# Reordering a turn of chunked linear attention: scores first, one row half for state and early value products

## The chip, the cores and the metric

The kernel runs on one core of a Trainium2 chip. The core has TensorE (PE, matmuls into PSUM), VectorE (DVE), ScalarE (ACT), GpSimdE (POOL), and SyncE (SP), which issues the transfers here. Each engine works through its own list in order; semaphores tie the lists together. The metric is the time of one execution on the device in microseconds (us).

## The reference, cut to what matters

A linear attention with a decaying state, then a dense MLP, then a mixture of experts. The change touches the attention alone:

```python
for t in range(S):
    kt, vt, rt = (k[:, :, t], v[:, :, t], r[:, :, t])
    cur = np.einsum('bhd,bhe->bhde', u[None] * kt, vt)
    y[:, :, t] = np.einsum('bhd,bhde->bhe', rt, state + cur)
    state = w[None, :, :, None] * state + np.einsum('bhd,bhe->bhde', kt, vt)
...
x = np.ascontiguousarray(attn_out.transpose(0, 2, 1, 3)).reshape(B * S, H * D)
x = _moe_ref(x=x, **moe_kwargs)
return _moe2_ref(x=x, **moe2_kwargs)
```

There are 4 batches, 8 heads, 768 tokens and a head dimension of 48; all matrices of the attention are fp32.

## The kernel before, in words

The tokens of a batch are cut into 6 chunks of 128, so there are 24 chunks, taken chunk by chunk over the 4 batches. r is scaled by falling powers of w (RT), k by rising ones (raw_p, KP in the code), so that inside a chunk the decay falls away: y of a chunk is scores times values, below the diagonal, plus a diagonal with u, plus RT times the state that came in. Heads are handled in four pairs j; s is the head in the pair. The first head of a pair has its 48 dimensions in partitions 0 to 47, the second in 64 to 111. Tokens come in two halves of 64 as well, so that most matmuls use one half of PE's rows and one half of its columns.

`turn(i)` issues the work of one step of the pipeline, and 25 turns run one after another, `merge`d with steps of the splitting of the MLP's weights (`load_weights`: mk and wah on ACT, four ti/tf steps on DVE, wal on POOL). PACE says how many steps each turn takes; a piece needs five, and a turn takes mostly four. On PE a turn consists of these blocks, named as the rest of this document names them:

- **state** (L436): RT of chunk i-1 times SW, the decayed state, into y
- **pk** (L402): transposes of the scaled k of chunk i+2; ACT copies the result to KT (`keep_k`)
- **kv** (L451): k times v of chunk i, which DVE adds to the state (Sn)
- **early products** (L464): those value products of chunk i-1 whose weights read the token half that lies in the first row half
- **sums** (L351): two columns per pair of u-weighted products of chunk i+1; ACT copies half of them to cs, then writes four diagonal blocks of AT (L368), and DVE the other four (`diagonal`)
- **late products** (L474): the value products with the other token half
- **scores** (L509): RT times KT of chunk i into pA

`masked` copies what is above the diagonal of pA over AT (a predicated copy on DVE) and the blocks between the token halves (on ACT). After the late products ACT copies y to ysb (L486), and SP writes that to DRAM (xd). y, pA, pk and kvc (kv and the sums) have one PSUM buffer each. Where two blocks write one bank of y from different row halves, `after` puts a drain on PE and waits for it:

```python
self.nc.tensor.drain().then_inc(self.tiles, 1)
self.nc.tensor.wait_ge(self.tiles, self.count)
```

State is left out in the first five turns (i up to 4), as the first chunk of each batch has none. `warm` issues matmuls of the identity whose result nobody reads. Ahead of turn 0 `att_setup` builds the powers TK and TR by doubling, and calls `warm` by the four numbers of WARM. Loads are issued by `load_chunk(i + 5)` after turn i.

Of the kernel before, what the change touches and what calls it, by code (L numbers as in the profile page):

```python
# [18 lines left out]
P = 128  # L19
# [4 lines left out]
NCB = S // P  # L24
# [20 lines left out]
EARLY = "k0 r0 k1 r1 w k2 r2 w k3 r3 w"  # L45
SLOTS = (0, 1, 2, 3, 5, 4, 7, 6)
WARM = (8, 10, 3, 2)
# [40 lines left out]
class Kernel:  # L88
# [20 lines left out]
    def consts(self):  # L109
# [6 lines left out]
        twice = cp.tile([P, P + 64], F32, name="ident")  # L116
        self.ident, self.swap = twice[:, :P], twice[:, 64:]
        v.tensor_scalar(self.ident, jp, 0.0, None, op0=ALU.is_equal)
        v.tensor_copy(twice[:, P:], twice[:, :64])
# [47 lines left out]
    def att_setup(self, ctx):  # L167
# [33 lines left out]
        for i in range(8):  # L201
            if i < 7:
                v.reciprocal(IW[:, i, :], PW[:, i, :])
                v.tensor_mul(PW[:, i + 1, :], PW[:, i, :], PW[:, i, :])
            if i == 0:
                g.tensor_copy(TR[:, :, 127], IW[:, 0, :])
            else:
                i -= 1
                n = 1 << i
                pb = PW[:, i, :].unsqueeze(2).to_broadcast([112, 4, n])  # L210
                ib = IW[:, i, :].unsqueeze(2).to_broadcast([112, 4, n])
                v.tensor_mul(TK[:, :, P - 2 * n:P - n], TK[:, :, P - n:], pb)
                g.tensor_mul(TR[:, :, P - 2 * n:P - n], TR[:, :, P - n:], ib)
# [5 lines left out]
        for j in range(4):  # L219
            if j < 2:  # L220
                nc.tensor.transpose(pt[:, j, :112], TK[:, j, :], self.ident[:112, :112])
            else:
                for c in range(2):
                    nc.tensor.matmul(pt[64 - 64 * c:P - 64 * c, j, :112], TK[:, j, 64 * c:64 * c + 64],
                                     self.ident[:112, :112], start=True, stop=True)
# [8 lines left out]
        self.kvc = self.pa.tile([P, 4 * D + H + 1], F32, tag="kv", name="kvc")  # L234
        self.pA = self.pa.tile([P, 2, 512], F32, tag="pA", name="pA")
        self.tiles, self.count = self.tc.alloc_semaphore("tiles"), 0
        self.scale_r(0)
        self.warm(WARM[2])
# [5 lines left out]
        self.warm(WARM[3])  # L244
# [36 lines left out]
    def warm(self, n, t=None):  # L281

        if n and t is None:
            t = self.pa.tile([P, P], F32, tag="kv", name="warm")
# [59 lines left out]
    def sums(self, prod, mark=False):  # L344
# [3 lines left out]
        for j in range(4):  # L348
            for c in range(2):
                d = 64 * (c if j < 2 else 1 - c)  # L350
                mm = self.nc.tensor.matmul(cc[d:d + 64, 2 * j:2 * j + 2], prod[:, j, 64 * c:64 * c + 64], self.uw[:, j, :],  # L351
                                           start=True, stop=True, skip_group_check=True)
                if mark and j == 0 and c:
                    self.ordered(mm)

    def diagonal(self, i):
# [6 lines left out]
        AT = self.AT[i] = self.wk.tile([P, 2, 384], F32, name="AT", bufs=3)  # L363
        sh = [P, 4, 64]
        nc.vector.tensor_tensor(AT[:, 1, :256].rearrange("p (j t) -> p j t", j=4), self.i64.unsqueeze(1).to_broadcast(sh),
                                cc[:, 1::2].unsqueeze(2).to_broadcast(sh), op=ALU.mult)
        for j in range(4):
            nc.scalar.mul(AT[:, 0, 64 * j:64 * j + 64], self.i64, cs[:, j:j + 1])  # L368
# [27 lines left out]
    def turn_k(self, i, **kw):  # L396
# [4 lines left out]
        for j in range(4):  # L401
            self.nc.tensor.transpose(pk[:, j, :], KP[:, j, :112], self.ident if j < 2 else self.swap)  # L402

    def keep_k(self, i):
# [3 lines left out]
        self.nc.scalar.copy(KT, self.pk)  # L408
# [7 lines left out]
    def turn(self, i):  # L416
# [6 lines left out]
        if cur:  # L423
            KV, KP = self.raw["k", i % NRAW["k"]], self.raw["p", i % NRAW["p"]]
        if prev:
            self.masked(i - 1)
            y = self.pa.tile([112, 2, 512], F32, tag="y", name="y")
            side = lambda j, s: 64 * (s if j < 2 else 1 - s)
            place = lambda j, s, o: y[side(j, s):64 if side(j, s) == 0 else 112, j // 2, P * (j % 2) + o:P * (j % 2) + P]
            width = lambda j, s: D if side(j, s) else 64  # L430
            RTp = self.RT.pop(i - 1)
            if pc:
                for j in (0, 2, 1, 3):
                    for s in range(2):
                        o = slice(64 * s, 64 * s + D)
                        nc.tensor.matmul(place(j, s, 0), self.SW[o, pb, j * D:j * D + width(j, s)], RTp[o, j, :],  # L436
                                         start=(j % 2 == 0), stop=False, skip_group_check=True)
# [4 lines left out]
        if prev and pc < NCB - 1:  # L442
            g.tensor_mul(self.SW[:, pb, :4 * D].rearrange("p (j d) -> p j d", j=4),
                         self.Sn[(i - 1) % 2].rearrange("p (j d) -> p j d", j=4), self.WC)
        kv = None
        if cur and c < NCB - 1:
            kv = self.kvc[:112, :4 * D]
            for j in range(4):
                for q, m in enumerate((64, D)):
                    h = 2 * j + q  # L450
                    mm = nc.tensor.matmul(kv[64 * q:64 * q + m, j * D:j * D + D], KP[:, h, :m], KV[:, h * D:h * D + D],  # L451
                                          start=True, stop=True, skip_group_check=True)
        yield
        prod = self.prod.pop(i + 1, None)
        if prev:
            Vp, ATp = self.raw["k", (i - 1) % NRAW["k"]], self.AT.pop(i - 1)
            if pc:
# [1028 lines left out]
```

## Time and profile before

| | |
|---|---|
| median of 3 runs | 855.35 us (854.48 to 858.29) |
| the profiled execution | 857.5 us |
| its span on the core | 855.7 us |
| mean granted clock of TensorE over the span | 0.898 |
| attention stage | to about 187 us of the span |

The span runs from the first to the last instruction that the profiler saw. The granted clock is a share of 2.4 GHz; its lower level, 1.2 GHz, reads 0.50. Matmul rows of one block overlap, so the length of a block is best read as the distance from its start to the start of the next. A product or transpose of fp32 may stand as more records than instructions.

### The profile page before, as it was taken

The numbers are of one execution on the slowest core, as the hardware profiler recorded it, in microseconds if no ns is written. First come the engines' busy times: TensorE is split into PE (matmuls) and PEld (weight loads), VectorE is DVE, ScalarE is ACT, GpSimd is POOL, SyncE is SP. The second block draws the span as 40 slices with busy tenths as digits, with TensorE's granted clock in tenths as the row PEclk, the third lists the DMA queues.
The fourth block names the chain that finished last, engine by engine and source line by source line (L and its number), as shares of the span: only waits on it lengthen the run. The fifth ranks groups of instructions, "written<-read, shape, count | busy, mean of one in ns | idle before, by whom it ended". The sixth has DMA issues, their size and how long they took to land.

```text
span 855.7 us, 17300 instructions
## 1 busy us (share of the span) xinstructions
PE 819.8 (96%) x6539; PEld 738.2 (86%) x6539; DVE 571.9 (67%) x1583; ACT 393.4 (46%) x861; POOL 269.3 (31%) x269
## 2 busy tenths in 40 slices
PE   8889899989999999999999999999899999999996
PEld 7777777768999999889999999998889999999996
DVE  5644544539879899998898843466868777875221
ACT  4543443446664444444444444563254544444441
POOL 6535335313230000000000000000295867777771
PEclk8655555559999999999999999999999999999998
DMA  8645346324502002002002001000553355327400
GB/s 250 160 149 172 110 142 184 120 59 148 171 15 74 1 1 75 0 10 93 28 20 83 11 1 56 1 21 10 170 191 115 97 196 205 129 91 233 159 29 29
DMA packets 56362, 81.42 MB, mean 95 GB/s; under 512 B 6990, under 2 KB 42064, under 8 KB 56144
## 3 DMA queue, kind: packets, MB, share of 16 engines
q1 hardware_dynamic: 53168, 70.81, 26.4%
q0 software_dynamic: 3104, 9.44, 3.3%
q8 instruction: 53, 0.87, 0.4%
q14 instruction: 37, 0.30, 0.1%
HBM read 66.08 MB, written 14.16 MB: 94 GB/s over the span
## 4 chain that ended last, share of the span: by engine, by line
PE 64%; DVE 5%; issue 3%; POOL 2%; ACT 2%; DMA 1%; POOLq 0%; ACTq 0%; DVEq 0%; SPq 0%
PE m L691 23%; PE ph L750 21%; PE eph L1238 8%; PE o L1255 8%; PE cnt L903 1%; DVE G L898 1%; POOL wal L1198 1%; PE ept L1222 1%; PE eph L286 1%; POOL wbl L1198 1%; DVE gh L765 1%; POOL out_dram L1268 1%; DMA xg<-md,idx 1%; ACT nt L754 0%; PE ip L1008 0%
## 5 line engine op out<-in xcount | busy, mean ns | idle before, releaser
L750 PE MATMUL ph<-xh,wah 128*128 128x512 f32 (+1 forms) x336 | 123.1, 366 | 1.0 <-ACTq L259 0.8
L750 PE MATMUL ph<-xh,wal 128*128 128x512 f32 (+1 forms) x336 | 122.7, 365 | 0.0
L750 PE MATMUL ph<-xl,wah 128*128 128x512 f32 (+1 forms) x336 | 122.7, 365 | 0.0
L691 PE MATMUL m<-wbh,gl 128*128 128x384 f32 (+1 forms) x352 | 119.3, 339 | 0.1
L691 PE MATMUL m<-wbl,gh 128*128 128x384 f32 (+1 forms) x352 | 119.2, 339 | 0.0
L691 PE MATMUL m<-wbh,gh 128*128 128x384 f32 (+1 forms) x352 | 119.1, 338 | 0.0
L754 ACT ACTIVATE nt<-ph 128x512 f32<-128x512 f32 (+1 forms) x112 | 60.1, 537 | 121.5 <-PE ph L750 115.5
L765 DVE SCALAR_TENSOR_TENSOR gt<-nt,al,gt 128x512 f32<-128x512 f32 (+1 forms) x96 | 67.7, 705 | 53.0 <-ACT gt L755 53.0
L773 ACT CAST gh<-gt 128x512 fp32r<-128x512 f32 (+1 forms) x96 | 56.4, 587 | 72.1 <-DVE gt L765 72.1
L147 POOL MEMSET io<- 128x1 f32 x1 | 0.1, 98 | 253.1 <-DVE io L146 253.1
L1241 ACT ACTIVATE hh<-eph 128x384 fp32r<-128x384 f32 x64 | 31.5, 492 | 103.8 <-PE eph L1238 99.8
L1246 DVE SCALAR_TENSOR_TENSOR hl<-eph,hh 128x384 fp32r<-128x384 f32 x64 | 35.4, 554 | 59.7 <-ACT hh L1241 59.4
L615 DVE SCALAR_TENSOR_TENSOR junk<-wt,wgb 128x384 f32<-128x384 f32 x128 | 71.3, 557 | 3.9
L750 PEld LDWEIGHTS ph<-xh,wal 128*128 128x128 f32 x336 | 63.8, 190 | 11.0
L750 PEld LDWEIGHTS ph<-xh,wah 128*128 128x128 f32 x336 | 63.7, 189 | 9.4 <-ACTq L259 0.9
L750 PEld LDWEIGHTS ph<-xl,wah 128*128 128x128 f32 x336 | 63.7, 190 | 7.7
L776 DVE TENSOR_TENSOR gl<-gt,gh 128x512 fp32r<-128x512 f32 (+1 forms) x96 | 61.7, 643 | 12.7 <-ACT gh L773 12.6
L691 PEld LDWEIGHTS m<-wbl,gh 128*128 128x128 f32 x352 | 66.1, 188 | 3.6
L691 PEld LDWEIGHTS m<-wbh,gh 128*128 128x128 f32 x352 | 66.1, 188 | 3.5
L691 PEld LDWEIGHTS m<-wbh,gl 128*128 128x128 f32 x352 | 66.1, 188 | 0.4 <-DVE gl L776 0.4
L1198 POOL TENSOR_TENSOR wbl<-raw,wbh 128x768 fp32r<-128x768 f32 x32 | 58.4, 1848 | 20.3 <-ACT wbh L1194 20.2
L1198 POOL TENSOR_TENSOR wal<-raw,wah 128x768 fp32r<-128x768 f32 x32 | 58.3, 1845 | 18.2 <-ACT wah L1194 17.0
(274 smaller groups left out, 1821.8 us busy)
## 6 DMA issues: line engine op xcount, KB each, us to landing
raw<-in_moe_w_dram SPq DMA_DIRECT2D x64, 384.0 KB, 5.8
raw_k<-in_kv_dram SPq DMA_DIRECT2D x24, 384.0 KB, 4.3
raw<-in_moe_w_in_dram SPq DMA_DIRECT2D x16, 384.0 KB, 4.3
raw<-in_moe_w_out_dram SPq DMA_DIRECT2D x16, 384.0 KB, 3.1
raw_r<-in_rt_dram SPq DMA_DIRECT2D x24, 224.0 KB, 4.5
xd<-ysb SPq DMA_DIRECT2D x48, 96.0 KB, 2.1
md<-raw SPq DMA_DIRECT2D x22, 192.0 KB, 2.0
xr<-xd SPq DMA_DIRECT2D x15, 256.0 KB, 4.0
```

Of the source, the lines that this page charges most:

```text
L615: v.scalar_tensor_tensor(junk, t, 1.0, self.wgb[:, e], op0=ALU.mult, op1=ALU.mult, accum_out=wc[:, f, e:e + 1])
L691: nc.tensor.matmul(acc[t][:, :N], a[:, o], self.wb[b][:, f, :N], start=(f == 0 and n == 0), stop=(f == NF - 1 and n == 2))
L750: nc.tensor.matmul(ph[:, :T], self.wa[a][:, k, fs], b[:, k, :T], start=(n == 0), stop=(n == 8))
L754: nc.scalar.activation(nt[:, :T], ph[:, :T], AF.Relu, scale=-1.0)
L765: v.scalar_tensor_tensor(gt[:, :T], nt[:, :T], self.al[:, f:f + 1], gt[:, :T], op0=ALU.mult, op1=ALU.add)
L773: nc.scalar.copy(h, g)
L776: v.tensor_sub(l, g, h.bitcast(F32))
L1198: self.nc.gpsimd.tensor_sub(to[1], d, to[0].bitcast(F32))
L1238: self.nc.tensor.matmul(ph, w1[a][:, k, f * P:(f + 1) * P], x[b][:, k], start=(n == 0), stop=(n == 8))
L1241: self.nc.scalar.activation(hh, ph, AF.Relu)
L1246: self.nc.vector.scalar_tensor_tensor(hl, ph, 0.0, hh.bitcast(F32), op0=ALU.max, op1=ALU.subtract)
L1255: self.nc.tensor.matmul(self.acc[q], h[a][:, o], w2[b][:, f], start=(f == 0 and n == 0), stop=(f == NS - 1 and n == 2))
```

## The change

Within a turn, scores(i) go from the end to the head, masked(i) follows in the same turn (before: masked(i-1) at the head of turn i), early products move up behind state, and sums stand ahead of kv. For the second head of each pair the two token halves of r, k and v are exchanged when the arrays are laid out, so that state and early products of one head use the same row half and the same bank of y; state of that head is issued in two pieces of 64 columns. The drains go, except in the last three turns. The late products, which come from the other row half, wait for the KT copy (`keep_k`) of the turn instead. AT and pA are laid out flat, so that one predicated copy of 512 elements does the work of two of 256. FILL adds 16 unread matmuls in turns 0 to 2. EARLY loads k and r of chunk 2 ahead of the first weight piece. The last doubling of TK and TR is split into a copy on ACT and two products each; `ident` replaces a second, shifted identity. In `scores` and `sums` only the places of the results differ.

```diff
-EARLY = "k0 r0 k1 r1 w k2 r2 w k3 r3 w"
-SLOTS = (0, 1, 2, 3, 5, 4, 7, 6)
-WARM = (8, 10, 3, 2)
+EARLY = "k0 r0 k1 r1 k2 r2 w k3 r3 w w"
+SLOTS = (0, 5, 2, 7, 1, 4, 3, 6)
+WARM = (8, 10, 4, 3)
+FILL = {(0, 0): 5, (0, 1): 3, (1, 0): 5, (2, 0): 3}
...
@@ -209,20 +208,20 @@
-                v.tensor_mul(TK[:, :, P - 2 * n:P - n], TK[:, :, P - n:], pb)
-                g.tensor_mul(TR[:, :, P - 2 * n:P - n], TR[:, :, P - n:], ib)
+                for e, t, b in ((v, TK, pb), (g, TR, ib)):
+                    if i < 6:
+                        e.tensor_mul(t[:, :, P - 2 * n:P - n], t[:, :, P - n:], b)
+                        continue
+                    nc.scalar.copy(t[64:, :, :64], t[64:, :, 64:])
+                    e.tensor_mul(t[:64, :, :64], t[:64, :, 64:], b[:64])
+                    e.tensor_mul(t[64:, :, 64:], t[64:, :, 64:], b[64:])
...
@@ -360,20 +358,22 @@
     def masked(self, i):
-        AT = self.AT[i]
-        sh = [P, 4, 64]
-        four = lambda t: t[:, :256].rearrange("p (j t) -> p j t", j=4)
-        for s in (1, 0):
-            self.nc.vector.copy_predicated(four(AT[:, s]), self.later.unsqueeze(1).to_broadcast(sh), four(self.pA[:, s]))
-            self.nc.scalar.copy(AT[:, s, 256:384], self.pA[:, s, 256:384])
+        if i >= NCH:
+            return
+        AT, pA = self.AT[i], self.pA
+        blocks = lambda t: t.rearrange("p (j t) -> p j t", t=64)
+        self.nc.vector.copy_predicated(blocks(AT[:, :512]), self.later.unsqueeze(1).to_broadcast([P, 8, 64]),
+                                       blocks(pA[:, 256:768]))
+        self.nc.scalar.copy(AT[64:, 512:], pA[64:, :256])
+        self.nc.scalar.copy(AT[:64, 512:], pA[:64, 768:])
...
@@ -420,67 +420,71 @@
+        fill = lambda k: self.warm(FILL.get((i, k), 0), self.kvc[:, 4 * D + H:])
+        if i:
+            self.scores(i)
         if prev:
-            self.masked(i - 1)
             y = self.pa.tile([112, 2, 512], F32, tag="y", name="y")
...
+                        for a, z, f, t in ((0, P, 0, P),) if not s else ((0, 64, 64, P), (64, P, 0, 64)):
+                            nc.tensor.matmul(place(j, s, a, z), self.SW[o, pb, j * D:j * D + width(j, s)], RTp[o, j, f:t],
+                                             start=(j % 2 == 0 and a == 0), stop=False, skip_group_check=True)
+            for j in (0, 2, 1, 3):
+                for s in range(2):
+                    r, h = slice(64 * s, 64 * s + 64), (2 * j + s) * D
+                    both = ATp[r].rearrange("p (n t) -> p n t", t=64)[:, j + 4 - 4 * s:9 + j:4 + 4 * s]
+                    nc.tensor.matmul(place(j, s, 0, P), Vp[r, h:h + width(j, s)], both,
+                                     start=(pc == 0 and j % 2 == 0), stop=False, skip_group_check=True)
+        self.scale_r(i + LOOK)
+        self.masked(i)
+        fill(0)
         self.turn_k(i + LOOK)
         self.scale_k(i + LOOK + 1)
-        self.keep_k(i + LOOK)
-        self.scale_r(i + LOOK)
...
+        kept = self.keep_k(i + LOOK)
+        yield
+        fill(1)
+        self.sums(self.prod.pop(i + 1, None))
         kv = None
...
+        self.diagonal(i + 1)
...
         if prev:
...
-            if pc:
+            if kept is None:
                 self.after()
...
             for j in (0, 2, 1, 3):
-                r = slice(64, P) if j < 2 else slice(0, 64)
                 for s in range(2):
-                    h = (2 * j + s) * D
-                    nc.tensor.matmul(place(j, s, 64), Vp[r, h:h + width(j, s)], ATp[r, s, 64 * j:64 * j + 64],
-                                     start=False, stop=True, skip_group_check=True)
+                    r, h = slice(64 - 64 * s, P - 64 * s), (2 * j + s) * D
+                    d = 256 * (1 - s) + 64 * j
+                    mm = nc.tensor.matmul(place(j, s, 64, P), Vp[r, h:h + width(j, s)], ATp[r, d:d + 64],
+                                          start=False, stop=True, skip_group_check=True)
+                    if kept is not None:
+                        self.tc.add_manual_dep(mm.ins, kept.ins.name, mybir.DependencyInfo(
+                            mybir.DependencyClass.Sync, mybir.DependencyReason.DATA), reason="two row tiles, one bank")
+                        kept = None
...
-        self.diagonal(i + 1)
-        yield
         self.product(i + LOOK)
+        yield
...
-        yield
-        if i:
-            self.scores(i)
...
@@ -1464,8 +1464,9 @@
-    kv = _np.concatenate([kv[..., :4, :], _np.roll(kv[..., 4:, :], 64, axis=2)], axis=4)
+    kv = _np.ascontiguousarray(_np.stack([v6, k6]).transpose(3, 1, 4, 0, 2, 5))
+    kv[..., 1::2, :] = _np.roll(kv[..., 1::2, :], 64, axis=2)
+    rt[:, :, 1] = _np.roll(rt[:, :, 1], 64, axis=4)
```

ACT in the middle of the stage, before, over one turn and more from a copy cs on; mk and wah are steps of the weights, AT<-i,cs are the diagonal blocks, AT<-pA the blocks between the token halves.

```order
L362 COPY cs<-kvc 128x4 [waits DVE_49]
L368 ACTIVATE AT<-i_78,cs 128x64 [waits Activation_49]
L368 ACTIVATE AT<-i_78,cs 128x64 x3
L531 ACTIVATE mk<-raw 128x384 [waits DMAHW1_49]
L486 COPY ysb<-y 112x512 [waits DMAHW7_49,DMAHW6_49,PE_49]
L376 COPY AT<-pA 128x128 [waits DVE_49] x2
L408 COPY KT<-pk 112x512 [waits PE_49,Pool_49]
L362 COPY cs<-kvc 128x4 [waits DVE_49]
L368 ACTIVATE AT<-i_78,cs 128x64 [waits Activation_49]
L368 ACTIVATE AT<-i_78,cs 128x64 x3
L544 CAST wah<-tf 128x3x128
L486 COPY ysb<-y 112x512 [waits DMAHW4_49,DMAHW3_49,PE_49]
```

ACT at the same place after, from the last diagonal blocks of a turn on.

```order
L366 ACTIVATE AT<-i_77,cs 128x64 x3
L531 ACTIVATE mk<-raw 128x384 [waits DMAHW1_49]
L490 COPY ysb<-y 112x512 [waits DMAHW7_49,DMAHW0_49,PE_49]
L375 COPY AT<-pA 64x256 [waits DVE_49]
L376 COPY AT<-pA 64x256
L408 COPY KT<-pk 112x512 [waits PE_49,Pool_49]
L360 COPY cs<-kvc 128x4 [waits PE_49]
L366 ACTIVATE AT<-i_77,cs 128x64 [waits Activation_49]
L366 ACTIVATE AT<-i_77,cs 128x64 x3
L544 CAST wah<-tf 128x3x128 [waits DVE_49]
L531 ACTIVATE mk<-raw 128x384 [waits DMAHW6_49]
L490 COPY ysb<-y 112x512 [waits DMAHW4_49,DMAHW3_49,PE_49]
```

cs waited for DVE before and waits for PE now, and KT stands behind two copies of 64x256. ysb still stands behind the diagonal blocks, with one weight step between them in the first of the turns shown and two in the second.

PE in the middle of the stage, before, from state on (y<-RT,SW is state, pk the transposes, kvc<-raw_k kv).

```order
L436 MATMUL y<-RT,SW 64x128 [waits Activation_49]
L436 MATMUL y<-RT,SW 48x128 x2
L436 MATMUL y<-RT,SW 64x128 x2
L436 MATMUL y<-RT,SW 48x128 x2
L436 MATMUL y<-RT,SW 64x128
L402 MATMUL pk<-ident,raw_p_119 112x128 [waits Pool_49]
L402 MATMUL pk<-ident,raw_p_119 112x128 x3
L451 MATMUL kvc<-raw_k_106,raw_p_115 64x48 [waits DMAHW1_49,DVE_49]
```

PE after, from the last columns of state on (y<-AT are the early products, kvc<-uw the sums).

```order
L437 MATMUL y<-RT,SW 48x64 x2
L437 MATMUL y<-RT,SW 48x128
L437 MATMUL y<-RT,SW 64x64 x2
L443 MATMUL y<-AT,raw_k_102 64x128
L443 MATMUL y<-AT,raw_k_102 48x128 x2
L443 MATMUL y<-AT,raw_k_102 64x128 x2
L443 MATMUL y<-AT,raw_k_102 48x128 x2
L443 MATMUL y<-AT,raw_k_102 64x128
L402 MATMUL pk<-ident,raw_p_114 112x128 [waits Pool_49]
L402 MATMUL pk<-ident,raw_p_114 112x128 x3
L351 MATMUL kvc<-uw,prod 64x2 [waits DVE_49,Pool_49]
L351 MATMUL kvc<-uw,prod 64x2 x7
```

The early products have moved up behind state and wait for nothing of their own, and the sums have moved up behind pk, ahead of kv.

PE further on in the turn, before: early products, sums, and the first of the late products; "tiles" is the drain.

```order
L464 MATMUL y<-AT,raw_k_105 64x128 [waits tiles,Activation_49]
L464 MATMUL y<-AT,raw_k_105 48x128 x2
L464 MATMUL y<-AT,raw_k_105 64x128 x2
L464 MATMUL y<-AT,raw_k_105 48x128 x2
L464 MATMUL y<-AT,raw_k_105 64x128
L351 MATMUL kvc<-uw,prod 64x2 [waits Pool_49]
L351 MATMUL kvc<-uw,prod 64x2 x7
L474 MATMUL y<-AT,raw_k_105 64x64 [waits tiles]
```

PE after, the late products, which stand behind kv.

```order
L475 MATMUL y<-AT,raw_k_102 64x64 [waits Activation_49]
L475 MATMUL y<-AT,raw_k_102 48x64 x2
L475 MATMUL y<-AT,raw_k_102 64x64 x2
L475 MATMUL y<-AT,raw_k_102 48x64 x2
L475 MATMUL y<-AT,raw_k_102 64x64
```

Both waits for a drain are gone; the late products wait for ACT, which is the KT copy of the turn.

## Rows read from the trace of the kernel before

**Rows 1.** The page, part 2: granted clock of TensorE in 40 slices, tenths.

```profile
PEclk8655555559999999999999999999999999999998
```

**Rows 2.** Windows: stretch, length, busy per engine (records), clock, DMA share, GB/s.

```profile
11.00:14.70 3.70, 3.20 (x68) 2.52 (x60) 1.52 (x6) 2.27 (x7) 2.28 (x2) 1.00 1.04 307
14.70:24.90 10.20, 8.93 (x136) 7.44 (x136) 6.26 (x14) 5.72 (x19) 6.34 (x7) 0.50 0.68 194
24.90:31.80 6.90, 4.82 (x148) 3.89 (x144) 4.55 (x10) 3.28 (x12) 3.71 (x4) 0.99 0.69 198
31.80:159.40 127.60, 116.12 (x1876) 93.79 (x1865) 61.28 (x132) 56.94 (x177) 58.24 (x63) 0.50 0.51 152
```

**Rows 3.** PE in order of time, first turns: start, length, ..., wait before and releaser.

```profile
5.04 2.50 PE L286 MATMUL warm<-ident 128*128 128x128 f32 x20
...
12.56 0.62 PE L402 MATMUL pk<-ident,raw_p 128*112 128x128 f32 x4 [0.20 <-ACT KT L408]
...
15.81 1.10 PE L402 MATMUL pk<-ident,raw_p 128*112 128x128 f32 x4 [1.36 <-POOL raw_p L387]
...
20.53 1.52 PE L509 MATMUL pA<-RT,KT 48*64 48x128 f32 x32
...
24.15 1.05 PE L464 MATMUL y<-AT,raw_k 64*64 64x128 f32 x16
...
26.15 0.86 PE L509 MATMUL pA<-RT,KT 48*64 48x128 f32 x32
26.94 0.65 PE L402 MATMUL pk<-ident,raw_p 128*112 128x128 f32 x4
27.52 0.67 PE L451 MATMUL kvc<-raw_k,raw_p 128*64 128x48 f32 x16
30.02 0.67 PE L464 MATMUL y<-AT,raw_k 64*64 64x128 f32 x16 [1.84 <-ACT AT L376]
30.62 0.63 PE L351 MATMUL kvc<-uw,prod 112*64 112x2 f32 x16
```

**Rows 4.** PE in order of time, one middle turn, and a start fifteen turns apart.

```profile
39.71 1.13 PE L436 MATMUL y<-RT,SW 48*64 48x128 f32 x16 [0.18 <-ACT ysb L486]
...
71.80 1.13 PE L436 MATMUL y<-RT,SW 48*64 48x128 f32 x16 [0.18 <-ACT ysb L486]
72.86 1.10 PE L402 MATMUL pk<-ident,raw_p 128*112 128x128 f32 x4
73.89 1.09 PE L451 MATMUL kvc<-raw_k,raw_p 128*64 128x48 f32 x16
75.23 1.13 PE L464 MATMUL y<-AT,raw_k 64*64 64x128 f32 x16 [0.25 <-PEq L380]
76.29 1.02 PE L351 MATMUL kvc<-uw,prod 112*64 112x2 f32 x16
77.43 0.71 PE L474 MATMUL y<-AT,raw_k 64*64 64x64 f32 x16
77.89 1.53 PE L509 MATMUL pA<-RT,KT 48*64 48x128 f32 x32
79.60 0.70 PE L436 MATMUL y<-RT,SW 48*64 48x128 f32 x8 [0.18 <-ACT ysb L486]
...
159.41 0.92 PE L436 MATMUL y<-RT,SW 48*64 48x128 f32 x12 [0.63 <-ACT ysb L486]
```

**Rows 5.** DVE and ACT in order of time, in that turn and the next.

```profile
77.43 0.36 DVE L478 TENSOR_TENSOR Sn<-kvc,SW 112x192 f32<-112x192 f32 x1 [3.15 <-PE kvc L351]
77.82 0.16 ACT L362 COPY cs<-kvc 128x4 f32<-128x4 f32 x1 [3.19 <-DVE Sn L478]
...
86.80 0.54 ACT L531 ACTIVATE mk<-raw 128x384 f32<-128x384 f32 x1
87.24 0.56 ACT L486 COPY ysb<-y 112x512 f32<-112x512 f32 x1
```

**Rows 6.** Windows: fifteen turns in one, columns as in rows 2.

```profile
39.71:159.41 119.70, 108.77 (x1740) 87.66 (x1740) 56.61 (x122) 51.78 (x160) 53.36 (x58) 0.50 0.50 150
```

More of the change, by code (lines that the diff above doesn't have):

```diff
@@ L219, in att_setup @@
         for j in range(4):
[L220 to L225, printed above, removed]
+            nc.tensor.transpose(pt[:, j, :112], TK[:, j, :], self.ident[:112, :112])
         self.TR = self.pa.tile([112, 4, P], F32, tag="TR", name="TRp")
@@ L243, in att_setup @@
         self.product(0, v)
-        self.warm(WARM[3])
+        self.warm(WARM[3], spare)
         self.scores(0)
@@ L283, in warm @@
         if n and t is None:
-            t = self.pa.tile([P, P], F32, tag="kv", name="warm")
+            t = self.pa.tile([P, P], F32, tag="pA", name="warm")
         for _ in range(n):
@@ L342, in load, with sums @@
                                {"k": self.kv, "r": self.rt}[n][c, b])
-    def sums(self, prod, mark=False):
+    def sums(self, prod):
         if prod is None:
@@ L349, in sums @@
             for c in range(2):
[L350 to L354, printed above, removed]
+                o = slice(64 * c, 64 * c + 64)
+                self.nc.tensor.matmul(cc[o, 2 * j:2 * j + 2], prod[:, j, o], self.uw[:, j, :], start=True, stop=True,
+                                      skip_group_check=True)
     def diagonal(self, i):
@@ L466, in turn @@
-        if prod is not None:
-            self.sums(prod)
-        if prev:
-            self.after()
-            for j in (0, 2, 1, 3):
-                r = slice(64, P) if j < 2 else slice(0, 64)
-                for s in range(2):
-                    h = (2 * j + s) * D
-                    nc.tensor.matmul(place(j, s, 64), Vp[r, h:h + width(j, s)], ATp[r, s, 64 * j:64 * j + 64],
-                                     start=False, stop=True, skip_group_check=True)
+                    r, h = slice(64 - 64 * s, P - 64 * s), (2 * j + s) * D
@@ L480, in turn @@
                 v.tensor_copy(self.Sn[i % 2], kv)
-        self.diagonal(i + 1)
+        self.product(i + LOOK)
         yield
-        self.product(i + LOOK)
         if prev:
@@ L499, in scores @@
         RT, KT = self.RT[i], self.KT.pop(i)
[L500 removed]
+        cols = self.pA.rearrange("p (n t) -> p n t", t=64)
+        for j in range(4):
             for late in range(2):
[L502 to L510 removed]
+                for s in range(2):
+                    o, half = slice(64 * s, 64 * s + D), late ^ s
+                    n = 8 - 8 * s + j
+                    k = slice(64 * half, 64 * half + 64)
+                    to = cols[k, 8 + j - 4 * s] if late else cols[k, n:n + 5:4]
+                    self.nc.tensor.matmul(to, KT[o, j, k], RT[o, j, k] if late else RT[o, j, :], start=True,
+                                          stop=True, skip_group_check=True)
     def weight_load(self, shape, src):
```

61 lines of the change are left out of this document (20 added, 41 removed).

## The prediction

> **What bounds the kernel now.** I read the page first. Its row of TensorE's (PE's) granted clock shows 8, 6 and then seven times 5 tenths in the first nine of forty slices, and 9 in all others but the last [rows 1]. Those nine slices are the attention stage, the only one that the change touches beside the set-up ahead of it. So I cut the stage into windows [rows 2]: from 31.80 to 159.40 us PE is busy 116.12 of 127.60 us, and its granted clock is 0.50, the lower of its two levels (1.2 GHz). The clock fell twice, at about 14.7 and 31.8 us, and came back once, at about 24.9 us, for a stretch of 6.90 us.
>
> What PE did before each of these is in its order of time [rows 3]. The fall at 14.7 lies in a wait of 1.36 us for POOL, which ends at 15.81 us. The fall at 31.8 follows a wait of 1.84 us for the masked copy of AT on ACT. Before the rise at 24.9 PE had gone from scores (20.53) over pk and kv into early products (24.15) with no wait named in a row. After that no turn is without one, and the clock stays down.
>
> A turn at 1.2 GHz is then read off block by block [rows 4]: state 71.80, pk 72.86, kv 73.89, early products 75.23, sums 76.29, late products 77.43, scores 77.89, next state 79.60. That is 7.80 us: 7.25 us of blocks (1.06, 1.03, 1.09, 1.06, 1.02, 0.46, 1.53), two drains (0.25 and 0.12) and 0.18 of waiting for the ysb copy. Some turns wait 0.63 there, as the one that starts at 159.41. Fifteen turns from 39.71 to 159.41 take 119.70 us, 7.98 each. Last, the chain on ACT that ends in that wait [rows 5], and what the other engines do in the same fifteen turns [rows 6].
>
> **The change, part by part.**
>
> *Drains and the wait for the masked copy.* Both drains go (0.37 us a turn), and early products no longer read an AT that was masked in the same turn. The 1.84 us kind of wait [rows 3] is gone. The late products now wait for the KT copy. It follows pk by one ACT copy of 512 elements, some 0.56 us by ysb's [rows 5], while sums and kv keep PE busy for 2.11 us at 1.2 GHz or 1.30 us at 2.4, so I cost it at nothing; if the copy starts late, everything past that cover is paid.
>
> *A new closed chain.* y has one PSUM buffer, so state of the next turn cannot start before ysb has copied it, and on ACT ysb stands behind cs and the four diagonal products. Now kv and sums stand just ahead of cs, in the order sums, kv. I take it that cs waits for kv, the last writer of its bank, as before it waited for Sn though its own operand was older [rows 5]. From the end of the block to the next state: 0.12 (77.31 to 77.43), then from cs at 77.82 to state at 79.60, 1.78; together 1.90. The loop is state, early, pk, sums, kv, then that chain.
>
> - At 2.4 GHz [rows 3] gives early 0.60 (30.02 to 30.62), pk 0.58, sums 0.63, kv 0.67, scores 0.79. Late has no such row; I take half of 0.46, 0.23. Nor has state; early, with as many columns, says 0.60, and 12/16 of scores, since state now has 12 instructions for 8, says 0.59. I take 0.60. PE's work is 4.10. The loop is 0.60+0.60+0.58+0.63+0.67+1.90 = 4.98.
> - At 1.2 GHz the loop is 1.06+1.06+1.03+1.02+1.09+1.90 = 7.16, but the work is 7.25, which then sets the turn. State by scores' price would be 1.15 (12/16 of 1.53), 0.09 more; the range holds that.
> - Between the diagonal products and ysb the new ACT order puts 1, 0, 1, 2, 1 casts of weights in five turns. One takes 0.44 (86.80 to 87.24, [rows 5]). So a turn takes 4.98, 5.42 or 5.86 at 2.4, mean 5.42, and 7.25, 7.60 or 8.04 at 1.2, mean 7.62.
>
> Against 7.98 a turn gains 2.56 us at 2.4 GHz and 0.36 at 1.2. If cs waits for the sums alone, the loop at 2.4 GHz is 0.67 shorter, 4.75 on the mean; that is its lower bound.
>
> *Other engines.* In fifteen turns DVE works 56.61 us, ACT 51.78 and POOL 53.36 [rows 6], at most 3.8 a turn. One masked copy of 512 elements takes the place of two of 256, and two AT copies of 64x256 that of two of 128x128; the first costs no more than what it replaces, the second at most two copies of 512 elements, 1.1 us. Even then ACT works 3.5+1.1 = 4.6 a turn, less than 5.42, so none of them bounds it. Nor do the loads: the stage moves 152 GB/s at 7.98 a turn, which is 224 at 5.42, and 307 was moved from 11.00 to 14.70 us [rows 2].
>
> *First five turns and the set-up.* Sixteen fill products at 0.25 us (10 products, shown as 20 records, in 2.50 us, [rows 3]) cost 4.0 us, inside the loop. With them the five turns without state take about 5x(0.60+0.58+0.63+0.67+1.90+0.44)+4.0 = 28.1 at 2.4 GHz, against 27.2 now (12.56 to 39.71, [rows 3, 4]). PE's work alone would be 5x3.50+4.0 = 21.5. I take no gain, between 0.9 us lost and 5.7 won. The split doubling of TK adds a copy and a product to its chain; the warm-up, which runs to 7.54 either way [rows 3], hides it in part or whole, and without that cover it would cost about 1 us once.
>
> **How much of the stage runs at 2.4 GHz** decides the sum. At 2.4 GHz a turn of 5.42 holds 4.10 us of work and one wait of 0.88, 1.32 or 1.76 us, between scores and state. The two waits before a fall were 1.36 and 1.84. So I expect turns with two casts to lose the clock, those with one to be borderline. At 1.2 GHz a turn without a cast runs late, scores, state, early, pk (5.1 us) with no wait, longer than the run ahead of the rise at 24.9; that comes one turn in five, while the others wait 0.35 or 0.79 there. The clock should thus alternate, with spells of a few turns at each level. The stage's end, where pk and kv run out, is likely slow. I take 0.4 of the turns at 2.4 GHz, between 0.1 and 0.7.
>
> A page bears on this in two places. The Trainium skill, TensorE: Matmul & The Clock Gate, "A second HAM failure mode: psum-queue depth-cycling", says that short PE idles between groups of matmuls make the clock go up and down between its two levels; the two falls agree, but no run here shows it as a steady state. The same page, "Part 4: PE-mode transpose", says that transposes do not count as busy in the way matmuls do. By that rule pk would lift nothing and the clock would stay down, which is the second rival with its 848; the rise at 24.9 came with a pk block of 1.03 us in the run before it, so the trace speaks against it without settling it.
>
> Sum for twenty turns with a state: 20x(0.4x2.56+0.6x0.36) = 24.8. From the profiled execution's 857.5 that leaves 832.7. The median of the runs shown is 2.15 lower, so I name **830.5** for a median. With 0.1 or 0.7 of the turns it is 843.7 or 817.3.
>
> **Rivals.**
> - *The clock holds through the stage.* For it: from 24.90 to 31.80 it held for 6.90 us with PE busy 4.82 of them [rows 2], 70%, where the new turn has 4.10 of 5.42, 76%. Against it: that stretch ended in a fall, and the new turn's longest wait is as long as the wait there. Twenty turns at 2.56: 51.2 less, 804.
> - *The clock stays at 1.2 GHz once the fills end.* For it: 127.60 us at 91% busy did not lift it [rows 2]. 20x0.36 = 7.2 less, 848.
> - *Nothing to measure:* the clock stays down, and the fills (4.0) and state at its upper price (20x0.09) eat most of the gain: 848.2+4.0+1.8 = 854.
> - *Slower: the KT copy becomes late.* On ACT it stands behind the two copies of the masked scores, they behind the masked copy, which on DVE stands behind Sn, up to two weight steps and RT. The late products, and with them ysb, then wait. At 1.2 GHz it takes over 0.36 us of such wait per turn to lose. With one weight step's worth, 0.54 by mk's [rows 5], a turn takes 8.16, and twenty lose 3.6; with state's upper price (1.8) and 0.9 in the first turns that is 862 as a median. It needs the masked copy to end about 2 us after pk, while DVE is busy only half of the time at this clock [rows 6].
>
> **How the numbers follow.** Alternating clock 0.55, held 0.20, down 0.13, nothing 0.07, slower 0.05. 0.5% (4.3 us) is about what a measurement of this kernel can tell from no change. The first three are faster, but the slow end of "down" is within 0.5%, so faster 0.86, same 0.09, slower 0.05. The range 806 to 850 leaves out half of the held clock at the low end and the last two cases at the high end.
>
> **What would show it.** In the profile after: granted clock near 0.7 in the stage, with stretches at both levels; turns near 5.4 us in the one and 7.6 in the other; a wait of state for ACT ysb of about 1 us at 2.4 GHz; no wait of early products for AT; the late products not waiting for KT. I am wrong if the clock is one level all through, if state starts at once behind scores (then the loop is not what I think), or if the time comes from the MLP stage, where I expect no difference.

## The result, and the profile after

The changed kernel takes **806.00 us** (median of four runs, 802.45 to 808.97), the kernel before 856.22 beside it. The ratio is 0.9411, with a 95% interval of 0.9357 to 0.9465: 50 us less, where 24.8 were forecast and 806 was the low end of the range. The profiled execution is the fastest of the four (802.45 us, span 800.7 us), so its account is made against the profiled 857.5 of before (span 855.7). Two of the four took 802.45 and 803.46 us with mean clocks of 0.995 and 0.998, two 808.55 and 808.97 with 0.981 and 0.978, and where these lost the clock no trace shows.

The page of the changed kernel, granted clock in 40 slices:

```profile
PEclk9999999999999999999999999999999999999998
```

The seven slices at 5 and the one at 6 [rows 1] are gone. The same windows as in rows 2, and fifteen turns from state to state as in rows 6 (stretch, length, busy per engine with records, clock, DMA share, GB/s):

```profile
11.00:14.70 3.70, 2.98 (x59) 2.49 (x59) 1.96 (x5) 1.81 (x7) 3.00 (x4) 1.00 1.05 327
14.70:24.90 10.20, 9.63 (x212) 8.63 (x211) 5.93 (x14) 5.92 (x18) 5.95 (x7) 1.00 0.55 154
24.90:31.80 6.90, 5.48 (x139) 4.47 (x138) 4.51 (x10) 4.64 (x14) 4.13 (x5) 1.00 0.75 207
31.80:120.00 88.20, 70.08 (x2128) 58.69 (x2130) 59.37 (x124) 63.75 (x188) 60.74 (x66) 1.00 0.77 228
39.34:115.19 75.85, 61.19 (x1861) 51.42 (x1861) 50.45 (x106) 53.95 (x158) 51.30 (x57) 1.00 0.78 230
```

The clock is 1.00 through all the turns, and low only for some 3 us at the start of the MLP (0.50 from 133.60 to 136.70 us). Fifteen turns take 75.85 us, 5.06 each, against 7.98 [rows 6]. PE is now busy for 61.19 of 75.85 us, less of its time than before, and yet at the higher level.

PE in order of time over a turn without a cast of weights and the starts of the next turns (start, length, what, wait before):

```profile
60.17 0.69 PE L437 MATMUL y<-RT,SW 48*64 48x128 f32 x23 [0.98 <-ACT ysb L490]
60.65 0.27 PE L443 MATMUL y<-AT,raw_k 64*64 64x128 f32 x2
...
60.70 0.63 PE L443 MATMUL y<-AT,raw_k 64*48 64x128 f32 x14
61.26 0.65 PE L402 MATMUL pk<-ident,raw_p 128*112 128x128 f32 x4
61.84 0.63 PE L351 MATMUL kvc<-uw,prod 112*64 112x2 f32 x16
62.32 0.64 PE L461 MATMUL kvc<-raw_k,raw_p 128*64 128x48 f32 x16
62.90 0.46 PE L475 MATMUL y<-AT,raw_k 64*64 64x64 f32 x16
63.16 1.07 PE L509 MATMUL pA<-RT,KT 48*64 48x64 f32 x32
64.80 0.69 PE L437 MATMUL y<-RT,SW 48*64 48x128 f32 x23 [0.57 <-ACT ysb L490]
...
69.89 0.69 PE L437 MATMUL y<-RT,SW 48*64 48x128 f32 x23 [1.02 <-ACT ysb L490]
...
75.37 0.33 PE L437 MATMUL y<-RT,SW 48*64 48x128 f32 x5 [1.41 <-ACT ysb L490]
...
109.53 0.69 PE L437 MATMUL y<-RT,SW 48*64 48x128 f32 x23 [0.58 <-ACT ysb L490]
...
111.69 0.65 PE L461 MATMUL kvc<-raw_k,raw_p 128*64 128x48 f32 x16
112.71 0.46 PE L475 MATMUL y<-AT,raw_k 64*64 64x64 f32 x16 [0.38 <-ACT KT L408]
...
115.19 0.69 PE L437 MATMUL y<-RT,SW 48*64 48x128 f32 x23 [1.14 <-ACT ysb L490]
...
133.59 0.80 PE L750 MATMUL ph<-xh,wah 128*128 128x512 f32 x1 [0.75 <-ACTq L259]
```

And ACT at the end of the first of these turns, and a copy cs of the turn that starts at 109.53:

```profile
63.02 0.16 ACT L360 COPY cs<-kvc 128x4 f32<-128x4 f32 x1 [0.44 <-PE kvc L461]
63.22 1.06 ACT L366 ACTIVATE AT<-i,cs 128x64 f32<-128x64 f32 x4
64.19 0.56 ACT L490 COPY ysb<-y 112x512 f32<-112x512 f32 x1
...
112.97 0.16 ACT L360 COPY cs<-kvc 128x4 f32<-128x4 f32 x1
```

The closed loop is there as forecast: cs waits for kv, the four diagonal products and ysb follow, and state waits for ysb in every turn shown. Turns of 4.63, 5.09 and 5.48 us follow from no, one and two casts between cs and ysb; there are 12 casts there in the fifteen turns, 0.8 a turn. The late products wait for KT only now and then (0.38 us at 112.71). Two of the fifteen turns take 5.65 and 5.66 us with one cast (the second from 109.53 to 115.19): ACT's copies of AT had waited for the masked copy on DVE, KT and a cast stand behind them, and cs came 1.28 us after the start of kv (111.69 to 112.97) where it otherwise comes 0.70 after it.

Where the 55.0 us of the two spans went: the first state starts at 39.34 for 39.71, 0.37; fifteen turns 119.70 - 75.85 = 43.85; the MLP's first product stands at 133.59 us of the span, before at 187.36, so the last turns gave 53.77 - 43.85 - 0.37 = 9.55; from there to the end 667.11 us for 668.34, 1.23. It is the turns.

### The profile page after: what moved, and what is told of

It is laid out like the page before. It is cut to its first block, busy times and chain, and to the rows that moved or that the text cites. A ratio compares the mean times of both kernels' runs of the same rounds, so it can differ in the third digit from the quotient of the medians.

```text
span 800.7 us, 17601 instructions
## 1 busy us (share of the span) xinstructions
PE 759.8 (95%) x6729; PEld 693.6 (87%) x6729; DVE 565.4 (71%) x1559; ACT 398.5 (50%) x863; POOL 270.4 (34%) x270
## 4 chain that ended last, share of the span: by engine, by line
PE 71%; DVE 5%; issue 3%; ACT 2%; POOL 2%; DMA 0%; POOLq 0%; ACTq 0%; DVEq 0%
PE m L691 25%; PE ph L750 24%; PE eph L1238 10%; PE o L1255 9%; PE cnt L903 1%; DVE G L898 1%; PE ept L1222 1%; PE eph L286 1%; DVE gh L765 1%; POOL out_dram L1268 1%; POOL wbl L1198 1%; ACT nt L754 1%; PE ip L1008 0%; DMA xg<-md,idx 0%; ACT gh L755 0%
```

## The experiments

The forecast allowed three cases for the clock: up, alternating, down. The questions were what holds it up, and whether the loop through ACT is the bound. "Changed" below is the changed kernel.

**No fill products.**

```diff
-FILL = {(0, 0): 5, (0, 1): 3, (1, 0): 5, (2, 0): 3}
+FILL = {}
```

> The changed kernel without its 16 fill products (five, three, five, three in the first three turns). Theory A (the fills carry the clock through the five turns without state, and a steady turn at 1.2 GHz, which has almost no wait but also twice the time per block, does not bring it back): the clock falls in the first turns and stays at 1.2 GHz; steady turns of 7.3 to 8.0 us, and 20 x (7.6 - 5.0) = 52 us less the fills' own time: 845 to 860. Theory B (a steady turn lifts the clock by itself; the fills only shorten the slow stretch at the start): clock low in the first turns alone, steady turns of 4.6 to 5.5 us, 804 to 815. Theory C (the fills are idle work): clock 1.0 all through, 802 to 806.

807.21 us, ratio 0.9426 (0.941 to 0.9441). Windows, and PE around the rise:

```profile
28.00:48.00 20.00, 19.66 (x324) 16.66 (x326) 10.02 (x22) 10.75 (x31) 11.68 (x13) 0.50 0.63 168
53.40:124.00 70.60, 57.11 (x1743) 47.99 (x1747) 47.94 (x100) 50.67 (x148) 49.22 (x54) 1.00 0.77 225
```

```profile
41.00 1.16 PE L437 MATMUL y<-RT,SW 48*64 48x128 f32 x24
...
48.02 0.81 PE L437 MATMUL y<-RT,SW 48*48 48x64 f32 x23
```

The clock fell at about 28 us and came back by itself at about 48, behind a turn with a state in which no row waits (41.00 to 48.02); nor does one in the turn ahead of it, from 34.72 on. Theory B is right. The fills spare 20 us at the low level in this trace; in the medians the difference (1.2 us) is inside the spread of the changed kernel's own runs.

**The old order with fills.** Before, plus five fill products ahead of pk in turn 1 and six ahead of the early products of turns 1 to 21.

```diff
+FILL = {(1, 0): 5, **{(i, 1): 6 for i in range(1, 22)}}
...
+        self.warm(FILL.get((i, 0), 0), self.kvc[:, 4 * D + H:])
...
+        self.warm(FILL.get((i, 1), 0), self.kvc[:, 4 * D + H:])
```

> The kernel before, in its old order and with its drains, with five fill products ahead of pk in turn 1 and six ahead of the early products of turns 1 to 21 (0.25 us each at 2.4 GHz, 1.5 us a turn, where early products wait for AT). It asks how much of the gain is the clock alone. Theory A (the level of the clock is most of the gain, and PE that is kept at work while it waits holds it): clock 1.0 in the stage, turns of about 4.10 us of blocks + 0.37 of drains + the AT wait of 1.84 or the fills that stand in it = 6.3 us, 20 x (7.98 - 6.3) = 33 us less than before, about 822. Theory B (the new order itself is needed to hold the clock): clock 0.5, and the fills, 3.0 us a turn at 1.2 GHz, stand on PE's own path: 20 x 2.5 = 50 us more, about 900.

874.18 us, with four runs from 856.66 to 879.16. PE over a turn that has the high level:

```profile
40.96 0.67 PE L437 MATMUL y<-RT,SW 48*64 48x128 f32 x16 [1.04 <-ACT ysb L489]
...
42.73 1.60 PE L287 MATMUL kvc<-ident 128*128 128x128 f32 x12
44.57 0.67 PE L467 MATMUL y<-AT,raw_k 64*64 64x128 f32 x16 [0.23 <-PEq L381]
...
48.10 0.67 PE L437 MATMUL y<-RT,SW 48*64 48x128 f32 x16 [1.04 <-ACT ysb L489]
```

This missed its question. I had taken the early products to wait for AT in every turn; here only the drain's 0.23 us stands ahead of them, so the fills stood on PE's own path, and the clock went up and down all the same. What it does show is the old order at 2.4 GHz: 7.14 us a turn with 1.60 of fills in it. Without them I estimate 5.5 us (7.14 - 1.60), and 6.0 for the turn that starts at 48.10 (the next state stands at 55.67); waits that the fills may have covered are not in that estimate. So the old order has a wait of over 1 us for ysb at that level as well, and a longer turn than the 4.63 to 5.48 of the new one.

**One, and two, more ACT copies ahead of ysb.** They lengthen the wait of state and take nothing away; the run with two has `range(2)`.

```diff
...
+            for _ in range(1):
+                nc.scalar.copy(self.junk[:, :, :112], self.TKm[:, :, :112])
             nc.scalar.copy(ysb.rearrange("p (a j) t -> p a (j t)", a=2), y[:, :, :2 * P])
```

> The changed kernel with one more ACT copy of 128x448 elements (0.5 us, of no use) ahead of each ysb copy. If the closed loop through ysb sets the turn, each turn is 0.5 us longer and the wait of state for ysb 1.1, 1.5 or 1.9 us where it is 0.57, 0.98 or 1.41. Theory A (the clock falls by one long wait, as the recorded prediction took it: 1.36 and 1.84 us stood ahead of the falls before): some turns now wait 1.9, the clock falls in the stage, 825 to 850. Theory B (one wait of that length does not make it fall while the rest of the turn has none): clock 1.0, 22 x 0.5 = 11 us more than the changed kernel, 813 to 818. If ysb is not on the loop: no difference to the changed kernel, 803 to 808.

> As the run with one more ACT copy ahead of ysb, but with two (1.0 us a turn): waits of state of about 1.55, 2.0 and 2.4 us at 2.4 GHz, turns of 5.6 to 6.5. Theory A (a long wait makes the clock fall): every turn waits longer than 1.36, so the clock falls in the first turns with a state and stays down or comes back for a turn at a time; at 1.2 GHz the loop is 7.2 + 1.0 = 8.2 to 9.0 us a turn, about the 7.98 of before or longer: 850 to 875. Theory B (length of the wait does not matter up to there): clock 1.0, 22 x 1.0 = 22 us more than the changed kernel, 825 to 830.

One copy: **836.03 us**, 0.9744 (0.9698 to 0.9791). Two: 861.81, 1.006 (1.004 to 1.008) of before. Windows of the run with one copy, the last from the first fall to the MLP:

```profile
77.90:91.60 13.70, 10.35 (x308) 8.56 (x306) 8.34 (x17) 9.71 (x28) 7.58 (x9) 1.00 0.69 196
91.60:95.00 3.40, 3.40 (x74) 3.06 (x70) 1.95 (x5) 2.47 (x9) 1.93 (x3) 0.51 0.53 178
95.00:112.10 17.10, 12.78 (x395) 10.70 (x397) 11.39 (x24) 13.36 (x37) 10.26 (x12) 1.00 0.77 216
112.10:129.10 17.00, 16.63 (x284) 13.72 (x274) 6.94 (x15) 8.68 (x25) 9.30 (x11) 0.50 0.52 142
...
37.00:163.15 126.15, 111.16 (x2354) 93.02 (x2349) 65.26 (x132) 81.14 (x225) 61.30 (x66) 0.66 0.57 164
```

PE around some of these, the starts of the states:

```profile
47.47 1.16 PE L438 MATMUL y<-RT,SW 48*64 48x128 f32 x24
...
55.14 1.16 PE L438 MATMUL y<-RT,SW 48*64 48x128 f32 x24 [0.41 <-ACT ysb L493]
...
78.06 0.69 PE L438 MATMUL y<-RT,SW 48*64 48x128 f32 x23
...
83.60 0.69 PE L438 MATMUL y<-RT,SW 48*64 48x128 f32 x23 [1.47 <-ACT ysb L493]
...
89.55 0.69 PE L438 MATMUL y<-RT,SW 48*64 48x128 f32 x23 [1.88 <-ACT ysb L493]
...
100.62 0.69 PE L438 MATMUL y<-RT,SW 48*64 48x128 f32 x23 [1.03 <-ACT ysb L493]
105.72 0.69 PE L438 MATMUL y<-RT,SW 48*64 48x128 f32 x23 [1.04 <-ACT ysb L493]
...
111.67 0.76 PE L438 MATMUL y<-RT,SW 48*64 48x128 f32 x23 [1.88 <-ACT ysb L493]
...
126.18 1.16 PE L438 MATMUL y<-RT,SW 48*64 48x128 f32 x24
```

At the high level the turns are 5.10 (100.62 to 105.72), 5.54 and 5.95 us. That is 0.1 us longer each than what was forecast for the change itself (4.98, 5.42, 5.86), and the clock alternates, as was forecast: it falls behind both waits of 1.88 shown, and 836 is the time. It comes back behind a turn without a wait at 78.06 and in the turn from 126.18, but a turn without a wait was not always enough: from 40.25 to 54.70 us PE was busy for 14.45 of 14.45 us, two turns on end (47.47 waits for nothing, 55.14 for 0.41), and the clock stayed at 0.50. What brings it back is thus not settled here. A mean of 0.66 in the last window is about a third of the time at the high level. With two copies the mean over the stage's turns, 31.80 to 190.00 us, was 0.56.

**The same two copies, ahead of the KT copy.** A long wait is split in two.

```diff
...
         KT = self.KT[i] = self.wk.tile([112, 4, P], F32, name="KT", bufs=3)
+        if i > LOOK:
+            for _ in range(2):
+                self.nc.scalar.copy(self.junk[:, :, :112], self.TKm[:, :, :112])
         return self.nc.scalar.copy(KT, self.pk)
```

> The changed kernel with the two useless ACT copies (0.5 us each) not ahead of ysb but ahead of the KT copy. KT then ends about 0.9 us after kv began to end, the late products wait 0.6 to 0.9 for it, cs and with it ysb move by as much, and state still waits 0.6 to 1.4: the turn at 2.4 GHz is 0.7 to 0.9 us longer than the changed kernel's 5.0, nearly as with two copies ahead of ysb (861.8), but its waiting lies in two pieces, neither above 1.45. Theory A (the clock falls by the longest single wait): no wait is longer than those that the changed kernel stands, so the clock holds, 22 x 0.8 = 18 us more, about 824. Theory B (it falls by how much of the turn is waited, in one piece or two): spells at 1.2 GHz as with the copies ahead of ysb, 835 to 862.

828.56 us, 0.9668 (0.9633 to 0.9704). One fall in its order of time on PE, and two waits further on that no fall followed:

```profile
60.59 0.46 PE L479 MATMUL y<-AT,raw_k 64*64 64x64 f32 x16 [1.01 <-ACT cs L361]
...
63.07 0.70 PE L441 MATMUL y<-RT,SW 48*64 48x128 f32 x23 [1.14 <-ACT ysb L494]
...
63.60 1.09 PE L447 MATMUL y<-AT,raw_k 64*48 64x128 f32 x14
...
86.67 0.46 PE L479 MATMUL y<-AT,raw_k 64*64 64x64 f32 x16 [1.01 <-ACT cs L361]
...
89.15 0.69 PE L441 MATMUL y<-RT,SW 48*64 48x128 f32 x23 [1.14 <-ACT ysb L494]
```

The clock fell behind waits of 1.01 and 1.14 us in one turn (the early products at 63.60 take the low level's 1.09). The changed kernel stood single waits of 1.41 and 1.14. So theory A, that the length of the longest wait decides, falls. The waits of one turn added up do not decide either: the same pair at 86.67 and 89.15 was followed by no fall, and from 80.38 to 111.00 us the clock read 1.00 with PE busy for 22.11 of 30.62 us. The time lies between the two forecasts, as the clock was down for only part of the turns.

**The longer wait, filled.** One copy ahead of ysb, and four fill products between scores and state:

```diff
...
         if prev:
+            self.warm(4, self.kvc[:, 4 * D + H:])
             y = self.pa.tile([112, 2, 512], F32, tag="y", name="y")
```

> The run with one useless ACT copy ahead of ysb (836.03), with four fill products on PE (0.25 to 0.27 us each at 2.4 GHz, about 1.05 us) between scores and state in every turn, where that run waits 1.04, 1.47 or 1.88 us for ysb. The loop keeps its length, and PE's idle time falls to at most 0.9 us a turn. Theory A (of the 30 us between that run and the changed kernel 22 x 0.46 = 10 us are the longer loop and the other 20 the spells at 1.2 GHz, which come from the idle time in a turn): the clock stays at 2.4 GHz, 816, between 812 and 822. Theory B (the spells come from the longer turn itself, or fill products do not count): the clock falls as before, and at 1.2 GHz 22 x 2.1 us of fills stand on PE's own path for the share of turns at that level: 845 to 870.

**814.66 us**, 0.9516 (0.9495 to 0.9537). Its window, and PE at the head of a turn, the fills and then state:

```profile
31.80:125.00 93.20, 86.09 (x2191) 73.11 (x2192) 56.86 (x120) 69.35 (x196) 58.19 (x65) 1.00 0.71 208
```

```profile
63.62 1.13 PE L287 MATMUL kvc<-ident 128*128 128x128 f32 x8 [0.28 <-DVE Sn L485]
64.79 0.69 PE L439 MATMUL y<-RT,SW 48*64 48x128 f32 x23
```

More work on PE, of no use to anyone, makes the kernel 21.4 us faster (836.03 - 814.66) with the same copy on ACT. So of the 30.0 us between one more ACT copy and the changed kernel, 8.7 (814.66 - 806.00) are the longer loop and 21.4 the spells at 1.2 GHz, and these come from PE's idle time in the turn, not from the turn's length (5.41 to 5.96 us from 59.27 to 87.22, for 5.10 to 5.95 at the high level without the fills). One rival stays: the fills use all rows and columns of PE, while a product of state, values or scores uses half of the rows and half of the columns at most, and whether as much work in the kernel's own small products would have held the clock was not tried.

**Shortening the loop.** Three edits to the changed kernel: both diagonal halves on DVE (no cs, no ACT products); the four ACT products behind ysb; a drain in place of the late products' wait for KT.

```diff
...
-            nc.scalar.mul(AT[:, 256 + 64 * j:320 + 64 * j], self.i64, cs[:, j:j + 1])
+        for q in range(2):
+            nc.vector.tensor_tensor(AT[:, 256 * q:256 * q + 256].rearrange("p (j t) -> p j t", j=4),
...
```

```diff
...
                     self.xd[:, tt * P:(tt + 1) * P].rearrange("(j s e) t -> s e j t", j=4, s=2)[s], ysb[q])
+        if i + 1 < NCH:
+            for j in range(4):
+                nc.scalar.mul(self.AT[i + 1][:, 256 + 64 * j:320 + 64 * j], self.i64, self.cs[:, j:j + 1])
```

```diff
-            if kept is None:
-                self.after()
+            kept = None
+            self.after()
```

> The changed kernel with the second half of the diagonal written by a second DVE product of 128x256 (0.42 us) in place of the cs copy and the four ACT products (1.06 us). If the closed loop through ACT is what sets the turn now, ysb stands behind the casts alone and waits for the late products: the turn falls from 5.0 us to PE's own 4.1 to 4.3, the wait of state for ysb is under 0.5 where two casts stand and none elsewhere, the clock stays at 2.4 GHz, 20 x 0.75 = 15 us less: 788 to 796. If the loop is not the bound (POOL's 3.45 us a turn, the loads at 228 GB/s or DVE set the turn): within 3 us of the changed kernel's 806. If DVE, which gets 0.42 us more a turn behind kv and ahead of Sn, RT and the masked copy, becomes the bound: 806 to 815.

> The changed kernel with the four ACT products of the diagonal behind the ysb copy of the turn in place of ahead of it (0.97 us off the way from cs to ysb, no work taken away). If the closed loop through ACT sets the turn: 4.1 to 4.3 us a turn, 788 to 797, and the AT copies of the next turn start later on ACT with nobody waiting. If only ACT's whole work counts (3.6 us of 5.0): no difference, 803 to 808. If AT comes too late for the masked copy and the early products: a wait of early products for AT and 806 to 825.

> The changed kernel with a drain of PE (as the kernel before had, 0.12 to 0.25 us) ahead of the late products in place of their wait for the KT copy. The late products are not on the closed loop (ysb stands behind the diagonal products on ACT, which end later): theory A, no difference to the changed kernel, 802 to 809, clock 0.98 or more. Theory B, PE's own work is what counts: 22 x 0.2 = 4 us more, 810. Theory C, the wait for KT (0.17 to 0.38 us in some turns) cost something: 2 to 4 us less, 802.

Diagonal on DVE: **797.84**, 0.9306 (0.927 to 0.9341), the fastest so far. Products behind ysb: 801.65, 0.9357 (0.9337 to 0.9378). In the second a spell at 1.2 GHz (49.3 to 57.5 us) took part of the gain, and its runs (800.47 to 804.72) overlap with those of the changed kernel; its turns at the high level are 4.72 us (18.88 us for the four from 61.56 to 80.44). Drain: 806.84, 0.9414 (0.9362 to 0.9466), no difference. Fifteen turns of the first, and two waits of its PE over the whole execution (us, times, longest):

```profile
41.95:112.78 70.83, 60.71 (x1848) 51.21 (x1844) 57.03 (x124) 37.31 (x84) 51.22 (x56) 1.00 0.83 249
```

```profile
PE y L473 <- ACT KT L406: 7.6, 10, 1.3
PE y L435 <- ACT ysb L488: 4.1, 6, 1.1
```

The loop was the bound: 4.72 us a turn for 5.06, half of what I expected. In place of the other half stands the late products' wait for KT, 5.2 us in seven of the fifteen turns. KT stands on ACT behind copies that wait for the masked copy on DVE. That is the step of the forecast's slower rival; it bites only now that the loop is shorter.

**Combinations**, to take that wait too: DVE diagonal with the drain; DVE diagonal with the KT copy ahead of the two AT copies; products behind ysb with the drain.

> Both diagonal halves on DVE (797.84 alone) and the drain of PE ahead of the late products in place of their wait for the KT copy (no difference alone). In the run with the diagonal on DVE the late products waited for KT ten times, 7.6 us in all, because the masked copy came late on DVE and the AT copies stand ahead of KT on ACT. If that wait is now what stands on the loop, it goes, and 22 drains of 0.1 to 0.2 us come: 4 to 6 us less, 791 to 794. If the loop waits anyway, a turn later, for the same masked copy (DVE is the bound): 796 to 799.

> Both diagonal halves on DVE (797.84 alone) and the KT copy ahead of the two AT copies on ACT. KT then follows pk at once, as the recorded prediction wanted it, and the wait of the late products for KT (7.6 us in all) goes without a drain; the AT copies move 0.5 us later and ysb with them where it stands right behind. If the late wait was on the loop: 790 to 794. If the AT copies, which wait for the masked copy, now hold the casts and ysb by as much: 796 to 800.

> The four ACT products of the diagonal behind ysb (801.65 alone, with 9.3 us of waits of the late products for KT and cs on ACT and a spell at 1.2 GHz at 48 to 58 us) and the drain in place of the wait for KT. If the late products' wait for KT is what gave back the gain and brought the clock down there (1.29 us ahead of the fall): clock 1.0, turns of 4.2 to 4.5 us, 790 to 796. If they wait for cs all the same (they must not write beside it): 800 to 804.

796.41 (0.9321, 0.9291 to 0.9352), 798.78 (0.9329, 0.9305 to 0.9352) and 802.38 (0.9394, 0.9374 to 0.9414): no gain over the two single edits. The wait for KT is gone in all three; state waits for ysb instead, 7.8 us in ten waits in the first, 6.5 in ten in the second and 9.6 in twelve in the third. What bounds a turn of 4.7 us I leave open: DVE with 57.03 of 70.83 us of work is the likeliest by the window above, but no run took work from it.

## Why the prediction was wrong

- **The change of order and the new loop: right in kind.** Its members, cs waiting for kv, and the wait of state for ysb are all in the trace. The casts are 12 in fifteen turns, 0.8 a turn where the pattern 1, 0, 1, 2, 1 has 1; the two turns with a late cs give about as much back. Early products wait for no AT.
- **Its size: the mis-sized term.** Forecast 0.60 + 0.60 + 0.58 + 0.63 + (0.67 + 0.12) + 1.78 = 4.98. Measured from start to start: state 0.48, early 0.61, pk 0.58, sums 0.48, kv to cs 0.70, cs to state 1.78, together 4.63. Sums and kv had been priced by the length of their records, which reach into the next block, though this document says ahead of the rows to go by starts; state, which had no row at this level, was taken as 0.60. A cast was right (4.63 to 5.09, 0.46 for 0.44). So the mean turn is 5.06, not 5.42, and the waits of state are about 0.57, 1.0 and 1.4 us in place of 0.88, 1.32 and 1.76.
- **The share of the turns at 2.4 GHz: the step that failed.** I took 0.4, writing "I expect turns with two casts to lose the clock, those with one to be borderline"; it was 1.0 in the profiled execution. The expectation is borne out for turns of about the size that I had put in: 0.1 us longer per turn, with one more ACT copy, it alternates and takes 836. So the 0.36 us per turn that I had over-priced cost the forecast twice: some 7 us as length (20 x 0.36), and more by tipping the clock. The reading behind it, that the length of one wait decides, was wrong as well: 1.41 us held here, 1.36 before did not [rows 3], and 1.01 with 1.14 in the same turn fell once and held once. What set these apart was not tried and stays open; the runs show only that the clock falls with idle time in the turn (filled, it holds) and that neither the longest wait nor the waits of one turn tell when.
- **The rival "the clock holds"** gave 804 and had 0.20. It was right about the clock, and in part by luck: it holds turns of 5.42 us, where the turns were 5.06, and its 51.2 us for twenty turns stand for 43.85 in fifteen and 9.55 in the last ones. The comparison that spoke for it, 76% of a turn at work against 70% in the stretch that held [rows 2], would not have carried: with one more copy the clock fell behind stretches with 76% (10.35 of 13.70 us) and 75% (12.78 of 17.10), and in the run with the split wait it held through one with 72% (22.11 of 30.62).
- **The rival "the clock stays down"** fails by the run without fills, where the clock came back unaided in turns with a state and, each turn with a pk block, held from 53.40 to 124.00 us. The Trainium skill, TensorE: Matmul & The Clock Gate, "Part 4: PE-mode transpose", says that transposes do not count as busy in the way matmuls do. The run without fills shows that this is no bar in turns that hold matmuls too; how much pk itself adds was not tried. The Trainium skill, TensorE: Matmul & The Clock Gate, "A second HAM failure mode: psum-queue depth-cycling", says that small idles between groups of matmuls make the clock alternate. The run with one more ACT copy agrees (0.66 as a mean, both levels within 37 to 163 us).
- **Nothing for other engines, loads and MLP:** right. The loads move 230 GB/s in the turns, the MLP gave 1.23 us. **First turns:** no gain, as taken (0.37 us).
- **The slower rival** (KT late) was not reached by its path: the late products wait 0.38 us for KT at most in a row shown, and a drain in place of the wait changes nothing. The late masked copy does cost some 0.57 us in two of fifteen turns, through cs, which stands behind KT and a cast on ACT.

The gain is thus mostly the clock. At 2.4 GHz I estimate the old order at 5.5 to 6.0 us a turn and measure the new at 5.06; the rest of the 2.92 us per turn is the level. That the old order could not have kept the level with turns of 5.5 to 6.0 us is argued from the run with one more copy, whose turns of 5.10 to 5.95 us lost it; no run shows it. Nor were the parts of the change run one by one: only the fills and the late products' wait were taken out alone, with no difference beyond the spread of the runs.

## What to carry to other kernels

Price a closed loop by the distances from start to start, not by the lengths of rows; with a clock that has two levels an error of 7% in the turn can decide between them, so work out on which side of the edge each end of your error bar lies. Where PE waits in every turn of a loop, neither the longest wait nor the share of work in one stretch was enough to tell here whether the clock stays up, so treat a turn that waits as one that may lose it. A few matmuls that nobody reads, put inside a wait that is there anyway, are a cheap test: if they make the kernel faster, the clock was the loss. After the loop has been shortened, look at what its old slack covered, here the KT copy behind the masked copy.

## What was not expected of the hardware

- PE was busy 91% of the time at 1.2 GHz for 127.6 us before [rows 2] without the clock coming back, and 81% of the time at 2.4 GHz (61.19 of 75.85 us) without it falling. The busy share alone thus did not tell the level.
- At 1.2 GHz the clock came back behind turns without any wait (34.72 to 48.02 us without fills; 70.84 to 78.06 with one more copy), but not behind all: with one more copy it stayed down from 40.25 to 54.70 us with PE busy throughout. Turns with even 0.18 us of wait and two drains, as before [rows 4], did not bring it back in fifteen turns.
- The same kernel can stand near the edge: with the drain, 809.13 us in its profiled execution, a wait of 1.40 us was followed by a fall (0.983 over the span), and four runs lay between 803.07 and 810.66.
